# A gated linear-attention and GEGLU kernel: another fixed order, with SyncE's issue of each DMA planned as a step, weights loaded in nine pieces, and a choice of engine for two elementwise steps

## Chip, cores, metric

One core of one Trainium2 chip; the calls of this study ran on different chips. The metric is the device time of one execution in microseconds (us), lower is better. Spans in traces are 1.7 us shorter than the device time of the same execution.

## The reference

Four batches of eight heads, 768 steps, head dimension 48. A complex-gated linear recurrence gives y, and y (3072 x 384) goes through a GEGLU block.

```python
mag = np.sqrt(a_re * a_re + a_im * a_im)
scale = np.minimum(mag, 0.999) / (mag + 1e-06)
for t in range(S):
    new_re = ar * S_re - ai * S_im
    new_im = ar * S_im + ai * S_re
    S_re, S_im = (new_re + k_t v_t^T, new_im)      # written short
    y[:, :, t] = q_t . S_re
g, val = x @ w_gate, x @ w_val                     # x is y, 384 -> 1536
return (gelu(g) * val) @ w_out                     # 1536 -> 384
```

## The kernel before

The kernel works in 24 chunks of 128 steps (six a batch) and in 8 units of three chunks (half a batch) for the gates. Log and angle of the gates are summed along time with triangular matrices on TensorE, turned into exponentials, sines and cosines, multiplied into q and k, and a chunk is then ordinary masked attention plus a state. Everything stands in one order, PLAN: each word is a step, a number after "=" is the buffer it writes, V or A the engine (VectorE or ScalarE). Each engine runs its own steps strictly in the order of the words.

```python
PLAN = """
ldare0=0 ldare1=1 tab.LE la0 ldaim0=0 r0=0 la1 ldaim1=1 r1=1 z0 ldv1=0 ldqk0=0 sq0 z1 ln0 vb1=0 ldqk2=1 sq1
...   # cut
gel4.0=1 g0.1=6 h2.1 g4.2=3 ldv8=1 h2.2 gel0.1=2 v4.0=5 pr5=2 gel4.1=0 tp6.0=0 ldqk9=3 sc3.1=6 v4.1=2
tps6.0A=0 h4.0=2 g0.2=4 ssb3.1=2 gel4.2=1 qk7=1 v4.2=5 vb8=7 tpd5.0=2 tp6.1=0 h4.1 y3.1 g0.0=6 tps6.1A=3 pr7=1
tpd5.1=1 v0.1=3 st6A=0 h4.2 sc6.0=2 x3A=1 v0.0=0 gel0.2=0 ssb6.0=1 ldv7=2 xtp3=5 gel0.0=1 v0.2=1 xt3A=1 h0.0=3
ldwo@qk9 sc6.1=4 y6.0=2 g3.1=6 ssb6.1=0 g3.0=5 h0.1 gel3.1=1 y6.1 sc5.0=0 h0.2 gel3.0=2 vb7=1 g3.2=4 x6A=0
...   # cut; dw7 stands in the next line
"""
FAST = (0, 1, 2, 3, 4, 5, 6,)     # units whose gates are loaded three steps a partition, in one DMA
SQUARES = (4, 6,)                 # units that take log(re^2 + im^2); the others log re and log(1 + (im/re)^2)

def load_weight(nm, after):       # "ldwo@qk9": w_out, behind the load of q and k of chunk 9
    t, src = WEIGHTS[nm]
    ...                           # cut: a one-column GpSimd copy that waits for the named load
    nc.gpsimd.dma_start(out=t, in_=src.rearrange("(c p) f -> p c f", p=128))

def si(u, slot, **_):             # im^2, for SQUARES
    nc.vector.tensor_tensor(out=take("s2", ("s2", u), slot), in0=T["aim", u], in1=T["aim", u], op=ALU.mult)

def vb(c, slot, **_):             # v to bf16
    nc.gpsimd.tensor_copy(out=take("vb", ("vb", c), slot), in_=T["v", c])

def tpd(c, hg, slot, **_):        # the pair of q and k of four heads, transposed by DMA
    src = T["pair", c][:, hg * 4:(hg + 1) * 4].rearrange("p h i s d -> p (h i s d)")
    nc.sync.dma_start_transpose(out=take("tps", ("tps", c, hg), slot), in_=src)

def dw(c, **_):                   # state update: pair^T v
    ...                           # cut: eight matmuls into the bank dwb, reading vb
```

Other words: la, r, sq, sr, ln are ScalarE steps of the gates (log, reciprocal, squares); z, ad, lx, mn VectorE ones; cum and cumt the sums on TensorE; ph, pg, sn phase, quarter turn and sine; tp a transpose on TensorE with copy tps; sc, ssb, y the attention; g, v, gel, h, fo, o the GEGLU block (g and v are its two up-projections, fo the down-projection); "tab.X" loads a table of ScalarE (LE log and exp, T arctangent and sine, G gelu); xtp or xtd transposes x on TensorE or by DMA.

Of the kernel before, what the change touches and what calls it, by code (L numbers as in the profile page):

```python
# [14 lines left out]
AF = mybir.ActivationFunctionType  # L15
ALU = mybir.AluOpType
# [9 lines left out]

PLAN = """
ldare0=0 ldare1=1 tab.LE la0 ldaim0=0 r0=0 la1 ldaim1=1 r1=1 z0 ldv1=0 ldqk0=0 sq0 z1 ln0 vb1=0 ldqk2=1 sq1
lx0=0 ln1 ldqk1=2 mn0 lx1=1 ldare3=0 tab.T at0=0 mn1 at1=1 cumt1=0 ldaim2=0 cumt0=1 ph1V=0 cumt5=2 pg1 ph0V=1
sn1=0 ldqk4=3 cumt2=3 pg0 ph5A=2 cumt3=4 sn0=1 pg5 cum0=5 ph3V=3 ph2A=0 cum4=6 sn5=2 ldqk6=4 pg2 cumt4=0 pg3  # L30
cum1=1 sn2=3 ph4V=1 cum5=2 sn3=4 cum2=3 pg4 ldaim3=1 cum3=4 sn4=5 tab.LE E0=0 ldare2=1 E2=1 qk0=0 E1=2 qk2=1
ldv0=1 E4=3 pr0=0 E5=4 ldv4=2 pr2=1 tp0.1=0 E3=5 ldwg@are2 la2 qk1=2 tp0.0=5 vb0=1 qk4=3 tp2.0=3 la3 vb4=2
pr1=2 dw0=0 r2=0 tp2.1=1 pr4=0 tps0.0A=0 z2 tp4.1=6 r3=1 sc0.0=2 tps2.1V=1 st0A=0 ssb0.0=0 sq2 tpd1.1=2
sc2.1=4 dw1 tps0.1V=3 tp4.0=5 st1A=1 y0.0=1 z3 sc0.1=2 ln2 tpd1.0=0 ssb0.1=1 sq3 lx2=0 y0.1 ldv3=3 tps2.0A=3
sc1.1=0 ldqk3=5 ssb2.1=2 x0A=0 sc2.0=2 mn2 ln3 ssb2.0=3 cum7=3 ssb1.1=0 sc1.0=4 cum8=1 E7=0 vb3=3 ldv2=4
ssb1.0=1 cum6=2 E8=1 lx3=1 y1.0=0 ldwv@v3 E6=2 y1.1 qk3=4 tps4.0V=0 vb2=4 tab.T at2=0 qk6=5 sc4.0=3 dw2 y2.0=4
pr3=2 at3=1 y2.1 cumt7=1 cumt8=2 ssb4.0=1 st2A=0 cumt6=5 ph7A=2 tps4.1V=2 dw3 ph8A=0 cumt9=3 ph6V=3 x1A=1
ldv6=5 cumt11=1 st3A=1 pg8 pg6 ph9A=1 sc4.1=6 xtp1=2 pg7 sn8=6 cumt10=0 tpd3.0=3 ssb4.1=0 dw4 y4.0=5 sn7=7
xt1V=0 x2V=1 y4.1 g1.1=3 ph10A=0 mn3 ldaim4=0 pg9 sn6=1 g1.0=6 vb6=5 ph11V=2 sn9=3 xtp2=2 pg10 g1.2=4 pg11
xt2V=1 sn10=0 v1.0=0 pr6=1 ldqk8=0 sn11=5 sc3.0=1 g2.2=2 x4V=1 st4V=1 g2.0=5 ssb3.0=3 dw6=0 ldqk5=1 si4=0  # L40
tab.G gel1.0=0 v1.1=1 gel1.1=1 v2.0=6 gel1.2=2 h1.0=0 g2.1=3 ldv5=0 qk8=6 gel2.2=0 v1.2=4 h1.1 xtd0=2 xtp4=0
v2.2=2 xt4A=0 pr8=0 tpd3.1=1 y3.0=1 gel2.0=1 v2.1=0 h1.2 g4.0=5 vb5=6 h2.0=1 gel2.1=2 ldqk7=2 g4.1=4 qk5=0
gel4.0=1 g0.1=6 h2.1 g4.2=3 ldv8=1 h2.2 gel0.1=2 v4.0=5 pr5=2 gel4.1=0 tp6.0=0 ldqk9=3 sc3.1=6 v4.1=2
tps6.0A=0 h4.0=2 g0.2=4 ssb3.1=2 gel4.2=1 qk7=1 v4.2=5 vb8=7 tpd5.0=2 tp6.1=0 h4.1 y3.1 g0.0=6 tps6.1A=3 pr7=1
tpd5.1=1 v0.1=3 st6A=0 h4.2 sc6.0=2 x3A=1 v0.0=0 gel0.2=0 ssb6.0=1 ldv7=2 xtp3=5 gel0.0=1 v0.2=1 xt3A=1 h0.0=3
ldwo@qk9 sc6.1=4 y6.0=2 g3.1=6 ssb6.1=0 g3.0=5 h0.1 gel3.1=1 y6.1 sc5.0=0 h0.2 gel3.0=2 vb7=1 g3.2=4 x6A=0
ssb5.0=3 v3.0=3 gel3.2=0 xtp6=6 v3.1=1 h3.0=4 sc5.1=5 xt6V=0 tp8.0=2 h3.1 v3.2=0 ssb5.1=2 y5.0=4 tps8.0V=0 dw7
tp8.1=3 ldare5=1 h3.2 y5.1 sc8.0=6 g6.1=1 st7A=1 tps8.1V=3 g6.2=5 x5V=1 gel6.1=2 ssb8.0=1 g6.0=2 tpd7.0=2
gel6.2=1 v6.1=0 gel6.0=0 xtp5=3 v6.0=4 tpd7.1=1 xt5A=2 sc8.1=1 g5.0=6 h6.0=5 ssb8.1=0 v6.2=5 ldare4=0 gel5.0=0
h6.1 g5.2=2 g5.1=3 h6.2 gel5.2=2 v5.0=4 gel5.1=1 ldqk10=5 v5.2=1 h5.0=6 v5.1=6 cum9=0 tab.LE la5 h5.1 ldaim5=1  # L50
fo0=5 h5.2 E9=3 r5=0 qk9=2 cum10=2 ldqk11=4 fo4=3 o0V=0 la4=1 pr9=2 E10=5 z5 ldqk12=0 r4 fo6=4 o4A=1 qk10=3
sq5 ldqk13=1 z4 fo3=6 o6A=2 sr4 pr10=1 ldout4 ln5 cum11=1 ad4 ldv10=3 fo1=0 E11=2 ldaim6=0 lx5=0 ln4=1 dw8
y8.0=5 qk11=4 tp10.0=2 o3A=1 y8.1 vb10=0 sc7.1=3 tps10.0A=0 mn5 tp10.1=4 ldv11=4 mn4 cum15=1 ssb7.1=3 st8A=1
cum17=6 ldv9=5 x8A=0 tps10.1V=3 cum16=2 E15=1 pr11=0 cum13=3 ldv17=0 E17=4 cum14=5 si6=0 cum12=4 vb11=4 xtd8=1
E16=0 fo2=1 ldv16=1 E12=3 vb9=2 E13=5 ldout6 qk12=5 vb17=3 ldout0 E14=2 sc7.0=6 sc10.0=2 qk13=6 sc10.1=4
ldaim7=1 fo5=3 ssb7.0=2 vb16=5 ssb10.1=1 tab.T at5=0 ssb10.0=0 y7.0=5 dw9 o2V=2 at4=1 y7.1 cumt16=6 o1V=0
ldv13=2 cumt17=4 st9V=0 ph16A=3 cumt15=2 tpd9.0=2 x7A=1 ph17V=1 y10.0=1 cumt14=0 ph15A=0 pg16 pg17 tp11.0=6
sn16=4 pg15 tp11.1=5 ph14V=2 ldv12=3 sn17=1 cumt13=4 vb13=6 tps11.0V=1 cumt12=2 ldout1 sn15=6 tps11.1V=0
xtp7=0 sc11.0=6 ldqk16=2 y10.1 pg14 ph12A=3 dw10 xt7V=0 g8.0=5 ph13A=1 ssb11.0=2 sn14=2 g7.0=2 pg12 vb12=7
pg13 o5A=0 sc11.1=0 x10V=0 ldv21=4 g7.2=4 sn13=7 ssb11.1=3 g8.2=6 sn12=3 ldv14=5 pr13=0 v8.0=3 xtd10=2 qk16=0  # L60
g7.1=1 ldqk15=3 v7.0=0 pr12=1 tab.G gel7.0=0 vb21=1 gel7.2=1 g8.1=2 h7.0=3 st10A=0 vb14=0 v7.1=4 gel7.1=2
tpd13.0=3 gel8.0=0 v8.2=0 h7.1 dw12=0 v7.2=1 h8.0=2 gel8.2=2 ldqk14=5 sc9.0=5 gel8.1=0 qk15=1 g10.0=4 y11.0=3
h7.2 v8.1=6 ssb9.0=0 tpd9.1=1 gel10.0=1 y11.1 v10.0=2 h8.1 x11A=1 y9.0=1 st12V=0 g10.1=5 h8.2 tpd13.1=0
xtp11=4 dw13 gel10.1=0 v10.1=3 qk14=2 g10.2=6 xt11V=0 ldqk17=4 h10.0=5 g11.2=0 gel10.2=2 pr16=2 g11.0=5
gel11.2=1 sc9.1=4 h10.1 g11.1=2 ldare7=1 ssb9.1=1 gel11.0=0 v11.2=6 pr14=0 y9.1 v11.1=0 st13A=1 qk17=3 x9A=0
sc13.0=3 v11.0=4 ssb13.0=2 xtp9=5 tpd12.1=2 dw14 v10.2=1 h11.0=4 sc13.1=3 xt9V=1 gel11.1=0 y13.0=4 h10.2
g9.0=5 tpd12.0=1 ssb13.1=3 g9.1=2 gel9.0=2 h11.1 g9.2=1 tpd14.1=3 h11.2 gel9.1=0 y13.1 v9.0=3 x13V=1 st14A=0
gel9.2=1 sc12.1=5 v9.1=0 h9.0=0 ldout5 ssb12.1=0 xtp13=2 tpd14.0=0 v9.2=6 xt13A=0 h9.1 sc12.0=4 g13.0=1 pr15=1
ldqk23=0 g13.2=3 gel13.0=2 ssb12.0=1 g13.1=5 gel13.2=0 h9.2 y12.0=2 v13.2=0 gel13.1=1 tpd15.1=1 y12.1 sc14.1=1
pr17=0 sc14.0=4 x12A=0 v13.0=3 ssb14.0=2 xtp12=6 v13.1=5 ldv15=0 xt12V=2 y14.0=2 ssb14.1=3 g12.1=4 ldv18=1  # L70
h13.0=1 g12.0=6 tpd15.0=2 h13.1 gel12.1=2 y14.1 g12.2=1 x14A=1 h13.2 vb15=4 gel12.0=1 v12.0=3 gel12.2=0
ldare6=0 xtp14=4 v12.2=5 h12.0=6 vb18=2 xt14A=1 v12.1=2 g14.1=0 h12.1 ldqk22=1 g14.2=6 gel14.1=1 h12.2 g14.0=1
gel14.2=2 fo8=3 gel14.0=0 ldout2 ldqk18=2 v14.1=4 tab.LE la7 o8V=0 v14.0=2 la6=0 tpd17.0=0 sc15.1=0 fo9=5
h14.0=2 ssb15.1=1 r7=1 h14.1 ldqk21=3 sr6 z7 fo7=6 r6 ad6 ldout3 sq7 fo13=1 ldqk19=5 o9V=2 z6 ln6=0 v14.2=3
ldout8 ln7 o13V=1 ldv22=2 fo12=2 mn6 h14.2 ldout13 lx7=1 ldqk20=4 cum18=0 cum19=4 o7V=0 E18=3 sc15.0=5 mn7
vb22=6 cum20=1 o12V=1 E19=5 ldv20=3 cum22=3 ssb15.0=0 cum23=6 E20=0 qk18=4 cum21=0 ldout12 dw15 fo14=2 E22=1
tpd16.0=3 qk19=6 st15A=1 qk22=5 E21=2 vb20=7 ldout9 y15.0=4 E23=4 qk20=0 fo10=5 tpd16.1=2 qk21=2 qk23=1 y15.1
tab.T at7=0 ldout7 fo11=1 o10V=1 tpd17.1=1 at6=1 x15V=0 o14V=2 sc16.0=3 xtd15=0 dw16 o11A=0 cumt22=0 ssb16.0=2
st16A=0 ldout14 sc17.0=6 cumt21=5 ph22A=0 cumt23=4 ssb17.0=3 ldv23=4 ph21A=2 sc16.1=2 pg22 cumt18=1 ph23A=1
pg21 sn22=0 ldout10 cumt19=3 ssb16.1=0 y16.0=0 ldout11 pg23 sn21=5 y17.0=5 cumt20=6 ph19V=3 ldv19=5 y16.1  # L80
sn23=7 ph18V=0 g15.0=4 vb23=0 pg19 ph20A=2 g15.2=2 x16V=1 sn19=3 pg20 sc17.1=3 xtd16=2 g15.1=1 pg18 sn20=4
ssb17.1=1 v15.2=6 pr19=1 sn18=2 vb19=4 y17.1 v15.1=0 x17V=0 tpd19.0=3 v15.0=3 pr18=2 g16.2=5 tab.G gel15.0=0
pr21=0 gel15.2=1 dw18=0 tpd19.1=0 g16.0=4 gel15.1=2 h15.0=0 v16.2=2 st18A=1 h15.1 gel16.2=0 v16.0=1 tpd18.0=2
h15.2 gel16.0=2 dw19 g16.1=3 st19V=0 fo15=5 xtd17=1 h16.0=3 gel16.1=1 tpd18.1=1 pr20=1 sc19.1=0 sc19.0=4
o15A=2 v16.1=6 ssb19.1=2 ldout15 ssb19.0=3 g17.1=1 h16.1 dw20 y19.0=3 gel17.1=2 v17.1=5 tpd20.1=3 h16.2
g17.2=0 pr23=2 y19.1 g17.0=4 gel17.2=1 x19V=1 tpd21.1=0 st20A=1 v17.2=6 gel17.0=0 sc18.1=1 sc18.0=2 dw21
ssb18.1=0 xtd19=0 fo16=0 ssb18.0=1 v17.0=3 o16V=1 sc21.1=4 y18.0=1 ldout16 h17.0=1 g19.0=2 tpd20.0=2 ssb21.1=3
g19.2=0 gel19.0=0 h17.1 v19.0=3 h17.2 gel19.2=2 y18.1 g19.1=4 tpd21.0=1 x18V=0 fo17=2 h19.0=6 gel19.1=1
xtd18=2 pr22=1 sc20.0=5 v19.2=0 o17V=0 v19.1=6 ssb20.0=2 ldout17 sc20.1=1 sc21.0=4 h19.1 y20.0=3 g18.0=2
# [8 lines left out]
ldout22 o23A=0 ldout23  # L98
"""

FAST = (0, 1, 2, 3, 4, 5, 6,)

SQUARES = (4, 6,)


@with_exitstack
def kernel(
# [148 lines left out]
    def si(u, slot, **_):  # L256
        nc.vector.tensor_tensor(out=take("s2", ("s2", u), slot), in0=T["aim", u], in1=T["aim", u],
                                op=ALU.mult)
# [223 lines left out]
```

## Time and profile before

| | before |
|---|---|
| time, median of the runs ahead of the prediction | 250.13 us (249.15 to 250.96) |
| profiled execution | 252.22 us, span 250.5 us |
| PE, DVE, ACT busy | 85%, 75%, 66% |
| DMA queue of SyncE | 140,032 packets, 38.4 MB, 80% of 16 engines' span |

The lines themselves are in the prediction. To read them: PE busy is not PE's useful work (at half clock the same matmuls are busy twice as long), so the prediction adds up the work at full clock, 197.5 us, and asks where the other 53 us of the span went. The profiled execution is labelled slow, which on one core means only that it is over 1.5% above the fastest run; no die or clock is set apart by it. What the slower runs have in common is looked at in the experiments.

### The profile page before, as it was taken

To read this page: it belongs to the slowest core of one execution; us is meant where nothing else is said; L and a number is where in the kernel's file an instruction comes from. 1 tells how busy PE (TensorE), PEld (TensorE's weight loads), DVE (VectorE), ACT (ScalarE), POOL (GpSimd) and SP (SyncE) were. 2 spreads that over 40 slices of the span, in tenths; PEclk is the share of its full clock that TensorE was granted. 3 is DMA by queue.
4 is the path that set the end of the run, shared out by engine and by line. 5 is a ranking of instruction groups with operands and counts; after the bars stand their busy time and mean duration, and the time that the engine had idled before them with its cause. 6 is when DMAs were issued, how large, how long until landed. Compare 5 with 4: busy or idle time off the path is not lost.

```text
span 250.5 us, 7144 instructions
## 1 busy us (share of the span) xinstructions
PE 211.8 (85%) x3006; PEld 178.3 (71%) x3006; DVE 186.9 (75%) x306; ACT 164.4 (66%) x256; POOL 27.2 (11%) x56
## 2 busy tenths in 40 slices
PE   0029267699997499999989999999999999999994
PEld 0015165479997497566889999866679888888892
DVE  4466699989997236999999997399979868454360
ACT  4998999898663049999894465796889321443221
POOL 8100311500110000033130000000000000000000
PEclk9999755789999689999999999999999999999999
DMA  7999799998979999579899999999975756873011
GB/s 206 277 261 221 198 185 190 182 226 163 185 116 187 156 220 228 117 182 225 179 190 149 203 175 159 221 194 256 194 194 97 152 119 132 133 85 100 16 34 63
DMA packets 142416, 42.41 MB, mean 169 GB/s; under 512 B 122672, under 2 KB 141616, under 8 KB 142384
## 3 DMA queue, kind: packets, MB, share of 16 engines
q1 hardware_dynamic: 140032, 38.42, 79.8%
q0 software_dynamic: 2352, 3.54, 8.6%
q8 instruction: 23, 0.38, 0.6%
q14 instruction: 9, 0.07, 0.1%
HBM read 30.67 MB, written 4.72 MB: 141 GB/s over the span
## 4 chain that ended last, share of the span: by engine, by line
PE 61%; DMA 13%; ACT 10%; DVE 8%; issue 3%; SPq 2%; POOL 0%; DVEq 0%; POOLq 0%
PE bank L400 30%; PE bank L423 16%; PE bank L288 6%; DMA v<-in_v_dram 5%; ACT cs L316 3%; PE bank L352 3%; DMA aim<-in_a_im_dram 3%; ACT L441 2%; DMA out_dram<-o 2%; DVE z L248 2%; DMA tps<-pair 2%; DVE qke L320 2%; DVE pair L329 1%; PE bank L368 1%; PE dwb L373 1%
## 5 line engine op out<-in xcount | busy, mean ns | idle before, releaser
L410 ACT ACTIVATE gel<-bank 128x512 bf16<-128x512 f32 x72 | 42.3, 600 | 46.9 <-PE bank L400 28.3
L416 DVE TENSOR_TENSOR h<-bank,gel 128x512 bf16<-128x512 f32 x72 | 48.0, 687 | 19.3 <-PE bank L400 18.8
L400 PE MATMUL bank<-xt,wg 128*128 128x128 bf16 x864 | 57.2, 222 | 1.5 <-ACT gel L410 1.1
L400 PE MATMUL bank<-xt,wv 128*128 128x128 bf16 x864 | 57.3, 219 | 0.0
L400 PEld LDWEIGHTS <-wg 128*128 128x128 bf16 x864 | 51.3, 99 | 1.9 <-issue 1.9
L400 PEld LDWEIGHTS <-wv 128*128 128x128 bf16 x864 | 50.4, 98 | 0.8
L423 PE MATMUL bank<-wo,h 128*128 128x384 bf16 x288 | 49.9, 326 | 0.0
L423 PEld LDWEIGHTS <-h 128*128 128x128 bf16 x288 | 27.4, 98 | 16.7
L355 DVE TENSOR_TENSOR ssb<-bank,tri 128x512 bf16<-128x512 f32 x48 | 32.3, 684 | 3.5 <-PE bank L352 3.3
L324 POOL CAST vb<-v 128x384 bf16<-128x384 f32 x24 | 18.0, 753 | 141.4 <-DMA v<-in_v_dram 112.4
L288 PEld LDWEIGHTS <-cum 128*128 128x128 bf16 x126 | 13.1, 108 | 27.0 <-issue 19.4
L288 PE MATMUL bank<-th,cum 128*128 128x384 bf16 x63 | 15.0, 388 | 17.7 <-ACT th L277 17.4
L329 DVE TENSOR_TENSOR pair<-qke,cs 128x768 bf16<-128x768 bf16 x48 | 25.8, 584 | 1.7 <-DMA tps<-pair 1.0
L320 DVE TENSOR_TENSOR qke<-qk,e 128x768 bf16<-128x768 f32 x24 | 23.3, 996 | 4.5 <-ACT e L299 3.6
L352 PE MATMUL bank<-tps 128*128 128x128 bf16 x192 | 19.2, 232 | 3.1 <-DVE tps L208 2.5
L316 ACT ACTIVATE cs<-ph 128x768 bf16<-128x768 int16 x24 | 18.9, 848 | 1.2 <-DVE ph L311 1.1
L352 PEld LDWEIGHTS <-tps 128*128 128x128 bf16 x192 | 13.5, 103 | 5.4 <-DVE tps L208 2.8
L338 PE MATMUL bank<-ident,pair 128*128 128x128 bf16 x112 | 11.0, 264 | 6.5 <-DVE pair L329 6.5
L368 PE MATMUL bank<-vb,ssb 128*128 128x48 bf16 x192 | 15.5, 187 | 0.9 <-DVE ssb L355 0.8
L441 ACT ACT_TABLE_LOAD x11 | 14.1, 1283 | 1.0 <-PEq L466 0.8
L298 ACT ACTIVATE e<-bank 128x384 bf16<-128x384 f32 x24 | 12.8, 532 | 2.8 <-PE bank L288 2.8
L208 ACT CAST st<-dwb 128x384 bf16<-128x384 f32 x16 | 7.9, 491 | 9.9 <-PE bank L368 9.4
(63 smaller groups left out, 248.9 us busy)
## 6 DMA issues: line engine op xcount, KB each, us to landing
v<-in_v_dram SPq DMA_DIRECT2D x24, 192.0 KB, 4.0
qk<-in_q_dram SPq DMA_DIRECT2D x24, 192.0 KB, 4.5
qk<-in_k_dram SPq DMA_DIRECT2D x24, 192.0 KB, 4.4
out_dram<-o SPq DMA_DIRECT2D x24, 192.0 KB, 2.6
are<-in_a_re_dram SPq DMA_DIRECT2D x7, 576.0 KB, 5.5
aim<-in_a_im_dram SPq DMA_DIRECT2D x7, 576.0 KB, 5.5
wg<-in_moe_w_gate_dram POOLq DMA_DIRECT2D x1, 1152.0 KB, 8.7
wv<-in_moe_w_val_dram POOLq DMA_DIRECT2D x1, 1152.0 KB, 9.9
```

Of the source, the lines that this page charges most:

```text
L288: nc.tensor.matmul(ps, mat, xin[:, :, c2, :], start=(n == 0), stop=(n == len(srcs) - 1))
L316: act(out=take("cs", ("cs", c), slot).rearrange("p s h d -> p (s h d)"), in_=lo[:, :, 0], func=AF.Sin, scale=2.0 * PI / TURN)
L320: nc.vector.tensor_tensor(out=take("qke", ("qke", c), slot), in0=T["qk", c], in1=T["e", c], op=ALU.mult)
L329: nc.vector.tensor_tensor(out=pair[:, :, i, :, 0:D], in0=T["qke", c][:, i].unsqueeze(2).to_broadcast([128, H, 2, D]), in1=T["cs", c].rearr ...
L352: nc.tensor.matmul(ps[:, hi, :], t[:, 2 * hi + 1, :], t[:, 2 * hi, :], start=True, stop=True)
L355: nc.vector.tensor_tensor(out=take("ssb", ("ssb", c, hg), slot), in0=T["sc", c, hg], in1=tri.unsqueeze(1).to_broadcast([128, 4, 128]), op= ...
L368: nc.tensor.matmul(ys, T["ssb", c, hg][:, hi, :], T["vb", c][:, h, :], start=first, stop=True)
L400: nc.tensor.matmul(ps[:, fi * L:(fi + 1) * L], w[:, i, fc * 128:(fc + 1) * 128], T["xt", c][:, i, :], start=(i == 0), stop=(i == NDM - 1))
L410: act(out=take("gel", ("gel", c, f), slot).rearrange("p a t -> p (a t)"), in_=T["g", c, f], func=AF.Gelu)
L416: nc.vector.tensor_tensor(out=T["h", c][:, f * FW:(f + 1) * FW, :].rearrange("p a t -> p (a t)"), in0=T["val", c, f], in1=T["gel", c, f].r ...
L423: nc.tensor.matmul(ps, T["h", c][:, fc, :], wo_sb[:, fc, :], start=(fc == 0), stop=(fc == NFF - 1))
L441: nc.scalar.preload_act_table_set(TABLES[word[4:]])
```

## The change

The intent: a planner that treats each DMA's issue on SyncE as a step with a duration makes the order, so that loads are not planned for times at which SyncE is still busy with other DMAs. It may also put the square of im and the quarter turn on either engine. Each weight is loaded in three pieces, other units take the log of re^2 + im^2 (SQUARES) or leave the interleaved load (FAST), and the new plan has 25 table loads in place of 11. The core of the diff (the plan is cut to its beginning):

```diff
 PLAN = """
-ldare0=0 ldare1=1 tab.LE la0 ldaim0=0 r0=0 la1 ldaim1=1 r1=1 z0 ldv1=0 ldqk0=0 sq0 z1 ln0 vb1=0 ldqk2=1 sq1
-lx0=0 ln1 ldqk1=2 mn0 lx1=1 ldare3=0 tab.T at0=0 mn1 at1=1 cumt1=0 ldaim2=0 cumt0=1 ph1V=0 cumt5=2 pg1 ph0V=1
+ldare0=0 ldaim0=0 ldare1=1 ldaim1=1 ldqk2=0 ldqk1=5 tab.LE la0=0 r0 ldqk0=4 sr0 z0 si0V=0 la1 ad0 ldaim2=0
+r1=1 ldqk3=3 ln0=0 z1 ldqk5=2 mn0 sq1 cum2=0 ln1 cum0=6 ldv0=0 cum1=5 E2=0 lx1=1 E0=5 ldqk4=1 E1=4 qk0=0
 ...   # cut: all other lines of the plan differ as well
-FAST = (0, 1, 2, 3, 4, 5, 6,)
-SQUARES = (4, 6,)
+FAST = (0, 1, 2, 3, 5,)
+SQUARES = (0, 2, 5, 6,)
-    def load_weight(nm, after):
+    def load_weight(nm, f, after):
         t, src = WEIGHTS[nm]
+        src = src.rearrange("(c p) f -> p c f", p=128)
+        if nm == "wo":
+            t, src = t[:, f * FW:(f + 1) * FW, :], src[:, f * FW:(f + 1) * FW, :]
+        else:
+            t, src = t[:, :, f * FW * 128:(f + 1) * FW * 128], src[:, :, f * FW * 128:(f + 1) * FW * 128]
-    def si(u, slot, **_):
+    def si(u, slot, eng):         # cut: eng "A" squares on ScalarE
-    def pg(c, **_):
+    def pg(c, eng, **_):          # cut: eng "A" turns on ScalarE
```

All 24 quarter turns and all four squares of the new plan stand on VectorE, so that choice is not used.

## The prediction

> **What bounds the kernel now.** I read four views of the kernel before, in this order. First the page's first two parts, busy shares and slices:
>
> ```profile
> PE 211.8 (85%) x3006; PEld 178.3 (71%) x3006; DVE 186.9 (75%) x306; ACT 164.4 (66%) x256; POOL 27.2 (11%) x56
> PE   0029267699997499999989999999999999999994
> ACT  4998999898663049999894465796889321443221
> PEclk9999755789999689999999999999999999999999
> DMA  7999799998979999579899999999975756873011
> ```
>
> PE is nearly full from the tenth slice (6.26 us each) to the end, with one hole in slices 13 and 14. So the bound is: a head of some 55 us in which PE has little to do, then PE itself. In the head ACT is at 9. To see what PE's work is worth without waits I took its durations from the chain: 12 matmuls of one up-projection group take 0.67 us, 12 of a down-projection 1.95, three of a 384-wide cumulative sum 0.49, eight transposes 0.45, four of a score 0.22, eight of a state update 0.20, and so on. By the plan's counts that is 144 x 0.67 + 24 x 1.95 + 138 x 0.163 + 14 x 0.45 + 48 x 0.22 + 20 x 0.20 + some 9 + 2 = 197.5 us. The span is 250.5, so 53 us are lost to PE. The stages show where (the columns after the stretch's length are PE, weight loads, DVE, ACT, POOL, then clock, DMA share, GB/s):
>
> ```profile
> 0.00:17.00 17.00, 0.00 (x0) 0.10 (x1) 9.47 (x13) 12.65 (x11) 6.61 (x27) 1.00 1.03 240
> 17.00:55.00 38.00, 27.07 (x243) 18.70 (x243) 30.12 (x49) 34.66 (x53) 6.95 (x9) 0.73 1.07 203
> 55.00:78.00 23.00, 23.00 (x432) 22.94 (x429) 21.83 (x39) 17.01 (x29) 2.29 (x4) 1.00 0.96 167
> 78.00:90.00 12.00, 7.14 (x101) 7.05 (x99) 4.55 (x9) 1.67 (x3) 0.51 (x1) 0.72 1.01 163
> 90.00:160.00 70.00, 68.91 (x1064) 59.83 (x1062) 60.48 (x98) 51.72 (x87) 8.81 (x11) 1.00 1.02 186
> ```
>
> Up to the first up-projection at 55.0 us only 18.6 us of the 197.5 are done: 36.4 us are lost there. The stretch 78 to 90 loses most of the rest; after 90 us PE is busy but for some 2 us, and the tail after the last matmul costs 3.6. Third, the waits of PE:
>
> ```profile
> PE bank L288 <- ACT th L277: 17.4, 1, 17.4
> PE bank L338 <- DVE pair L329: 6.5, 2, 4.9
> PE dwb L373 <- POOL vb L324: 4.9, 1, 4.9
> PE bank L352 <- DVE tps L208: 2.5, 2, 2.0
> ```
>
> The first two are the head: PE waits 17.4 us for the first arctangent and later for the first pair. The third is the hole. Fourth, the chain of work over the hole:
>
> ```profile
> 70.94 0.69 PE bank L400 x12
> 71.63 0.55 SPq L345
> 72.23 11.66 DMA v<-in_v_dram
> ...
> 84.02 0.52 POOL vb L324
> 84.54 0.04 issue
> 84.58 0.48 PE dwb L373 x8
> ```
>
> It is the load of v7: SyncE is in the middle of a transposing DMA (L345) until 72.2, only then issues v7, and this load lands after 11.66 us where the median is 4.0, because the weight load of w_out was issued at 70.97 and takes 12.7. PE waits 4.86 us and then runs at half clock: the eight matmuls of dw take 0.48 us instead of 0.20, the next eight transposes 0.85 instead of 0.45, the 48 up-projections 4.15 instead of 2.68. With the y and score matmuls between (some 0.4) that is 4.9 + 2.5 = **7.4 us lost to one late load**.
>
> **What the Trainium skill says.** "TensorE: Matmul & The Clock Gate", section "HAM oscillation — how this bites in real kernels": a PE gap longer than about 3.4 us brings the slow clock back. The trace agrees: clock 0.53 in 84 to 90 us after the 4.86 us wait, and 0.50 in 30 to 42 after the 4.9 us wait for the pair. "DMA: Bandwidth & Descriptors", section "Issuing engines are not separate DMA queues": transfers of all issuers share the same 16 DMA engines and interleave. The trace agrees: v7 took 11.66 us beside a 1152 KB weight load. "ScalarE: Activation LUTs", section "What ACT_TABLE_LOAD costs": about 1283 ns, plus a drain of about 1380. This trace has the first figure (11 loads, mean 1283 ns) but no second: the load at 14.89 us is followed by the arctangent at 16.18.
>
> **The change, part by part.** (1) The loads are placed earlier. I counted, for each load, the PE work that stands in the order between it and its first consumer. For v the median goes from 3.0 us to 9.1, for q and k from 6.1 to 13.5, for a_im from 4.1 to 7.2. v7, which stood 2.8 us ahead of its cast and 6.7 ahead of its matmul, now stands 11.3 and 36.2 ahead. In the order up to that matmul, six transposing DMAs of the pair become two, so SyncE isn't held by waits for pairs. The weights come in nine pieces of 384 KB instead of three of 1152, each behind some other load, so none can hold the DMA engines for 12 us. I expect the hole to go: **-7.4 us**.
>
> (2) Head. Units 0 and 2 now take the log of re^2 + im^2, so the first sum of logs doesn't wait for the quotient and its square: by the ACT and DVE durations (1.16 and 1.36 us) I get the first PE work near 13 us instead of 17.4, the exponentials of chunks 0 to 2 before the first table change, and the first pair near 23 to 25 instead of 29.2. The bound of this stretch is ACT, which ran some 4 us behind its own sum of durations before (51.0 us of work at 55.0). Before the first up-projection the new order has 48.3 us of ACT work against 51.0, with 19.9 us of PE work done against 18.6: ahead by 2.7 + 1.3 = 4. But at the first gelu table it has 55.3 against 53.5, with 26.1 of PE against 21.9: ahead by 2.4. And DVE has 52.4 us of work up to that place, against 44.2, because of the squares and adds of units 0 and 2 and the copies of transposes that PE now makes; it starts near 6 us and waits for ACT some 4 us, so both engines arrive at about 60 with no slack between them. I take **-1.5 us**.
>
> (3) PE's own sum. Units 4 and 6 leave the interleaved form: 138 cumulative matmuls become 126, -12 x 0.163 = -2.0 us. Pair transposes on PE go from 14 to 18, +4 x 0.45 = +1.8; those of x from 12 to 8, -4 x 0.17 = -0.7. Sum **-0.9 us**.
>
> (4) Table loads go from 11 to 25: 14 x 1.28 = +17.9 us on ACT, and the copies that move add nearly nothing. The new ones lie in pairs around single sines, logs or exponentials amid the gelus. There ACT has slack: from the second gelu stretch to the last a-units, 37.7 us of PE work stand beside 34.4 us of ACT. But each pair holds the gelus up for about 2.6 to 3.7 us while seven banks fill, so some of the seven new visits will cost PE some tenths. I take **+2.0 us**. DVE gains about 2 x (1.36 + 1.36 - 1.40) = 2.6 for squares plus some copies, beside PE.
>
> The choice of engine for quarter turn and square is not used by this plan: all of both stand on VectorE, so it costs nothing. The leave of the interleaved form adds 8 plain DMAs with short rows (q, k and v have the same rows and land in 4 us); they have much lead.
>
> Sum: 250.1 - 7.4 - 1.5 - 0.9 + 2.0 = 242.3, and I put 242.5.
>
> **The rivals.** First: another load is late in place of v7. For it: the DMA engines are already at 9 in most slices of the first 180 us, and the new order asks for 12.3 MB in place of 11.7 by the time 20 us of PE work are done, which at 215 GB/s is 57 us; the first piece of w_gate hangs behind q and k of chunk 6. Against: the leads above. If it comes, 5 to 8 us return: 247 to 250. Second: ACT becomes the bound amid the gelus. For it: 25 loads and a sum of 192 us by durations against 175. Against: in both orders the stretches where ACT is full (before: 96 to 126 and 161 to 190 us) have no more ACT work than before. If it does: +4 to +6, some 247. Third: the head follows its ACT sum fully and the extra tables hide: 237 to 239.
>
> **Range and chances.** The hole is sure to have cost 7 us, the head can go 4 us either way, table loads from 0 to 6. Range 236 to 249. Faster by over 2% means under 245.1: 0.68. Within 2%: 0.28. Slower: 0.04.
>
> **What would show it.** In the profile after: no PE wait for vb above 1 us and no clock under 0.9 after 60 us (part 1); first matmul near 13 us and first up-projection near 53 (part 2); 126 cumulative matmuls, 144 pair transposes (part 3); 25 table loads, and PE idle in front of gelus (waits of L400 on gel, now 1.1 us) of 2 to 4 us (part 4). A wait of several us on a load or on a weight piece, or ACT at 9 between 130 and 160 us, would prove me wrong.

## The result, and the profile after

The changed kernel took 243.05 us in the median (241.97 to 243.19, 4 runs) against 250.5 us (249.15 to 250.96) for the kernel before on the same chip. The ratio of the fast runs is 0.970, 95% interval 0.965 to 0.975. A ratio is the mean time of one kernel's fast runs over that of the other's of the same rounds, so not quite the ratio of the medians quoted. All four runs of before counted as fast there; the experiments show that this was the slower of two groups into which its runs fall.

The page of the changed kernel, busy shares and slices (6.03 us each):

```profile
PE 208.3 (86%) x3014; PEld 174.2 (72%) x3014; DVE 188.4 (78%) x308; ACT 180.5 (75%) x270; POOL 31.0 (13%) x68
PE   0058834999999999998999979999799999999993
ACT  3897899899769569699979869798899772333230
PEclk9999995699999999999999999999999999999999
DMA  7999999999897999999997999999957897601212
```

The hole of slices 13 and 14 is gone, PE's clock is full from the ninth slice on, and PE is at 5 in the third slice, where it was at 2. ACT is busier, 180.5 us against 164.4. The stages, cut as before (columns: length, then PE, weight loads, DVE, ACT and POOL with counts, clock, DMA share, GB/s):

```profile
0.00:17.00 17.00, 3.04 (x9) 1.38 (x10) 10.45 (x14) 12.41 (x15) 5.75 (x26) 1.00 1.02 243
17.00:55.00 38.00, 27.82 (x297) 19.78 (x297) 34.36 (x59) 34.95 (x53) 11.59 (x18) 0.87 1.12 221
55.00:78.00 23.00, 22.04 (x404) 21.48 (x403) 22.94 (x37) 19.53 (x29) 6.30 (x10) 1.00 0.89 167
78.00:90.00 12.00, 12.00 (x204) 11.24 (x202) 7.87 (x14) 6.92 (x12) 1.88 (x4) 1.00 1.14 179
90.00:160.00 70.00, 67.59 (x1011) 57.27 (x1009) 58.29 (x96) 61.34 (x93) 4.97 (x9) 1.00 1.03 189
```

In 78 to 90 us PE went from 7.14 to 12.00 us busy, with the clock from 0.72 to 1.00. In 55 to 78 it is DVE that is full, 22.94 of 23. The waits of PE (us in total, times, longest):

```profile
PE bank L299 <- DVE lx L285: 16.3, 3, 13.2
PE bank L382 <- DVE ssb L369: 3.1, 1, 3.1
PE bank L380 <- ACT st L211: 2.0, 1, 2.0
PE bank L366 <- DMA tps<-pair: 1.9, 2, 1.7
PE bank L414 <- DMA xt<-x: 1.3, 1, 1.3
```

The wait for vb is not among them. The first wait now ends at 13.2 us with a sum of logs, where the first arctangent ended it at 17.4. No wait for a gelu shows; transposing DMAs (3.2 us) are new.

Loads do still land late. The landings of the q and k loads, of before and then of the changed kernel:

```profile
DMA to landing us min/median/max: 3.2/4.4/6.3
```

```profile
DMA to landing us min/median/max: 3.1/4.0/11.5
```

By the trace, four of them, issued between 43.0 and 46.3 us, took 8.3 to 11.5 us while pieces of w_gate and w_val were under way. With the lead that they have here VectorE waited 0.4 us for one q or k load in the whole run, and PE for none.

To say what each stage gave, take one mark that both have, the first down-projection. It is the start in the first line of the tile w_out (min, median and max ns, first and last start in us), here of before and then of the changed kernel:

```profile
L423 PE MATMUL bank<-wo,h x288: 322/326/326, 96.9 to 246.5; 128*128 128x384 bf16 x144
```

```profile
L437 PE MATMUL bank<-wo,h x288: 322/326/326, 88.5 to 237.1; 128*128 128x384 bf16 x144
```

By the durations in the prediction 51.7 us of PE work stand ahead of that mark in the order before and 52.8 in the new one, so 45.2 and 35.7 us were lost up to it: 9.5 us less. After the mark, before loses 153.6 - 145.8 = 7.8 us and the changed kernel 152.7 - 143.8 = 8.9: 1.1 us more. With 0.9 us less work in all that is 9.5 - 1.1 + 0.9 = 9.3 us, the difference of the spans.

### The profile page after: what moved, and what is told of

The parts are those of the page before. It is cut to its first block, busy times and chain, and to the rows that moved or that the text cites. A ratio compares the mean times of both kernels' runs of the same rounds, so it can differ in the third digit from the quotient of the medians.

```text
span 241.2 us, 7177 instructions
## 1 busy us (share of the span) xinstructions
PE 208.3 (86%) x3014; PEld 174.2 (72%) x3014; DVE 188.4 (78%) x308; ACT 180.5 (75%) x270; POOL 31.0 (13%) x68
## 4 chain that ended last, share of the span: by engine, by line
PE 60%; DVE 15%; ACT 10%; DMA 5%; issue 3%; SPq 1%; DVEq 0%; ACTq 0%
PE bank L414 32%; PE bank L437 15%; PE bank L299 6%; DMA tps<-pair 4%; PE bank L366 3%; DVE ssb L369 3%; DVE qke L334 2%; ACT e L310 2%; DVE pair L343 2%; ACT e L309 2%; DVE h L430 2%; DVE tps L211 1%; ACT L455 1%; ACT th L288 1%; ACT cs L330 1%
## 5 line engine op out<-in xcount | busy, mean ns | idle before, releaser
L424 ACT ACTIVATE gel<-bank 128x512 bf16<-128x512 f32 x72 | 40.9, 599 | 35.1 <-PE bank L414 16.7
L430 DVE TENSOR_TENSOR h<-bank,gel 128x512 bf16<-128x512 f32 x72 | 47.7, 685 | 17.9 <-PE bank L414 10.8
L414 PEld LDWEIGHTS <-wg 128*128 128x128 bf16 x864 | 50.2, 98 | 2.7 <-DMA xt<-x 1.4
L455 ACT ACT_TABLE_LOAD x25 | 32.1, 1283 | 1.2 <-PEq L480 0.8
L299 PEld LDWEIGHTS <-cum 128*128 128x128 bf16 x90 | 9.6, 115 | 25.1 <-issue 19.6
L299 PE MATMUL bank<-lx,cum 128*128 128x384 bf16 x45 | 12.8, 415 | 16.3 <-DVE lx L285 16.3
L338 POOL CAST vb<-v 128x384 bf16<-128x384 f32 x24 | 14.1, 618 | 97.6 <-DMA v<-in_v_dram 84.6
L343 DVE TENSOR_TENSOR pair<-qke,cs 128x768 bf16<-128x768 bf16 x48 | 24.4, 551 | 0.4 <-ACT cs L330 0.4
L366 PE MATMUL bank<-tps 128*128 128x128 bf16 x192 | 17.7, 222 | 3.3 <-DMA tps<-pair 1.9
L366 PEld LDWEIGHTS <-tps 128*128 128x128 bf16 x192 | 12.4, 99 | 6.1 <-DMA tps<-pair 3.7
L382 PEld LDWEIGHTS <-ssb 128*128 128x128 bf16 x192 | 12.0, 98 | 6.3 <-DVE ssb L369 3.5
L380 PE MATMUL bank<-st,tps 128*128 128x48 bf16 x160 | 13.9, 186 | 2.0 <-ACT st L211 2.0
```

Of the source, the lines that this page charges most:

```text
L299: nc.tensor.matmul(ps, mat, xin[:, :, c2, :], start=(n == 0), stop=(n == len(srcs) - 1))
L343: nc.vector.tensor_tensor(out=pair[:, :, i, :, 0:D], in0=T["qke", c][:, i].unsqueeze(2).to_broadcast([128, H, 2, D]), in1=T["cs", c].rearr ...
L366: nc.tensor.matmul(ps[:, hi, :], t[:, 2 * hi + 1, :], t[:, 2 * hi, :], start=True, stop=True)
L382: nc.tensor.matmul(ys, T["ssb", c, hg][:, hi, :], T["vb", c][:, h, :], start=first, stop=True)
L414: nc.tensor.matmul(ps[:, fi * L:(fi + 1) * L], w[:, i, fc * 128:(fc + 1) * 128], T["xt", c][:, i, :], start=(i == 0), stop=(i == NDM - 1))
L424: act(out=take("gel", ("gel", c, f), slot).rearrange("p a t -> p (a t)"), in_=T["g", c, f], func=AF.Gelu)
```

## The experiments

Words of the plan are moved unless said otherwise. Times are medians of all runs; the runs of before that shared the chip are given beside them.

### One load earlier

```diff
-... vb8=7 tpd5.0=2 ... tpd5.1=1 ... ssb6.0=1 ldv7=2 xtp3=5 ...
+... vb8=7 ldv7=2 tpd5.0=2 ... tpd5.1=1 ... ssb6.0=1 xtp3=5 ...
```

> The order of before with one word moved: the load of v7 stands ahead of the first transposing DMA of chunk 5 instead of behind the second, some 7 us of PE work earlier. Theory of the prediction (one late load cost 7.4 us): v7 issues near 67 us, lands before the w_out load starts, PE does not wait for vb, the clock stays 1.0 in 78 to 90 us, and the time falls by 6 to 8 us to some 243. Rival (the DMA engines are full and the hole only moves to another load or transpose): 247 or more, with a new PE wait of some us between 70 and 100 us.

Measured: 246.54 us (245.05 to 247.7, 4 runs), but before itself ran at 246.53 in the median there, 245.37 to 250.59 in 8 runs; the ratio of fast runs is 1.00, unclear. In the trace the hole is gone, as the stage and the tile w_out show:

```profile
78.00:90.00 12.00, 12.00 (x219) 11.60 (x217) 8.30 (x15) 6.81 (x10) 0.00 (x0) 1.00 1.25 209
```

```profile
L418 PE MATMUL bank<-wo,h x288: 322/326/326, 89.4 to 240.6; 128*128 128x384 bf16 x144
```

The longest landing of a v load fell from 11.7 to 6.5 us, and the first down-projection came 7.5 us earlier, at 89.4. The span is 5.9 us shorter than in the trace of before (244.6 against 250.5): 1.6 us were given back to other waits after the mark. So the mechanism stands. The time is not the 243 us that was expected and equals that of before, which was quick in five of its eight runs there. The likely reading, not shown, is that the hole is missing in those five.

### The weight later

```diff
-... h0.0=3 ldwo@qk9 sc6.1=4 ... gel3.0=2 vb7=1 g3.2=4 ...
+... h0.0=3 sc6.1=4 ... gel3.0=2 vb7=1 ldwo@v7 g3.2=4 ...
```

> The order of before, v7 issued as late as there, but the 1152 KB load of w_out hangs behind v7 instead of behind chunk 9's q and k. If the contention with w_out made v7 late (prediction): v7 lands in some 4 us near 76, no PE wait for vb, some 243 to 245. Rival (SyncE's late issue alone is the cause, or transposes hold the engines as well): v7 still takes over 8 us and the time stays at 248 to 250. A third way: w_out now comes late for the first down-projection at 97 us; then a PE wait on L423 shows.

Measured: 246.64 us (244.92 to 249.39, 4 runs), the same runs of before. SyncE issued v7 at 72.33 as late as before, behind the same two transposing DMAs; its cast ran at 75.44, so it had landed within 3.2 us:

```profile
72.33 0.58 SPq L213 DMA_DIRECT2D v<-in_v_dram  x1
75.44 0.51 POOL L319 CAST vb<-v 128x384 bf16<-128x384 f32 x1 [4.03 <-PE bank L395]
```

No wait for vb, first down-projection at 89.3, none for w_out. So it takes both: SyncE's late issue alone does no harm, and beside w_out v7 lands 7 to 9 us later. That is the prediction's reading, though the time is again above the 243 to 245 expected. One of the four runs took 249.39 us; it was not profiled, so what made it slow is open.

### The weight in three pieces at the same place

```diff
-ldwg@are2 ... ldwv@v3 ... ldwo@qk9
+ldwg0@are2 ldwg1@are2 ldwg2@are2 ... ldwv0@v3 ldwv1@v3 ldwv2@v3 ... ldwo0@qk9 ldwo1@qk9 ldwo2@qk9
```

(with the change's load_weight)

> The order of before with each weight loaded in three pieces of 384 KB as in the change, but all three pieces at the place of the whole. The same bytes at the same time: by the prediction v7 shares the engines with them as before, takes 9 to 12 us, and the time stays at 249 to 251. Rival (it is the size of one transfer that holds v7 back): v7 lands in under 7 us, PE waits less than 2 us, and the time falls to some 244.

Measured: 250.46 us (246.81 to 251.25, 4 runs). The time is what the prediction expected and the reason is not: no v load took over 6.8 us, as the rival said. What was lost is elsewhere. GpSimd issues the weights, a piece of w_gate takes it 1.7 us or more (a one-column copy and 0.8 to 0.9 us of issue), and three of them in a row hold the cast of v0 and v4 from 30.6 to 35.2 us. PE waits 2.6 us for vb in the head (1.6 behind the pieces of w_gate, 1.0 behind those of w_val), and the first up-projection starts at 57.4 instead of 55.0:

```profile
PE dwb L373 <- POOL vb L324: 2.6, 2, 1.6
```

v7 was issued 0.08 us behind the first piece of w_out and landed in 5.8 us; a load of a_re issued 0.6 us later still took 12.1 us (12.4 in before). So smaller pieces saved v7 here, not every load, and they cost GpSimd's queue; the time cannot be attributed to either alone.

### Whole weights in the new order

```diff
-... ldwg1@v1 ... ldwg2@v2 ... ldwv0@v9 ... ldwg0@qk6 ... (nine pieces)
+... ldwg@v1 ... ldwv@v9 ... ldwo@v10 ... (three weights whole, with the load_weight of before)
```

> The changed kernel with each weight loaded whole, at the place of the first of its three pieces. If the greater lead of the loads protects it (prediction): within 1 or 2 us of the changed kernel, 243 to 245, with no PE wait on vb over 1 us. Rival (spreading the weights in thirds is what removed the hole): a PE wait on a load of 4 us or more and 247 to 250.

Measured: 243.99 us (241.88 to 245.43, 4 runs). One v load (v9, whose issue began 0.4 us ahead of w_gate's) took 11.3 us here too. GpSimd holds w_val and the casts behind it until v9 has landed, and PE waited 0.5 us for a cast:

```profile
DMA to landing us min/median/max: 3.0/3.9/11.3
```

```profile
PE dwb L376 <- POOL vb L327: 0.5, 1, 0.5
```

The lead of the loads is enough to remove the hole; the splitting of the weights is not needed for it.

### The kernel before, once more

> The kernel before, unchanged, for a second trace: its runs so far lie from 245 to 252 us. If the late load of v7 is what tells its quick executions from its slow ones, a profiled run under 247.5 us shows no PE wait for vb over 1 us and a v7 landing in under 7 us, and one over 249 us shows the wait of some 5 us again. If the spread has another cause (clock, head), the wait is there in both.

The profiled run was of the slower group again (251.71 us). Its chain of work:

```profile
73.26 0.55 SPq L345
73.87 10.17 DMA v<-in_v_dram
...
84.16 0.52 POOL vb L324
84.72 0.41 PE dwb L373 x8
```

The same late load, with a PE wait of 3.4 us. The 68 timed runs of before in this study fall in two groups: 28 between 245.1 and 248.0 us (median 246.4), 37 between 249.0 and 253.3 (median 250.3), three between. The kernel with v7 earlier took 245.1 to 247.7 in its four runs, which is the quicker group. Both profiles of before fell in the slower group and show the hole. A quick execution was never profiled, so that the quick ones lack the hole is inferred from the edit, not seen. In the two traces w_out is issued at 70.97 and 73.32 us, 1.3 and 0.6 us before v7. That is close, but no trace shows the order turned round, and v9 above was late though its issue began 0.4 us ahead of w_gate's. One run with w_out later took 249.39 us as well. So what tells the two groups apart is not shown: the late load is the likely cause, and perhaps not the only one.

The label slow (over 1.5% above the fastest run) falls on most of the slower group, so the ratio of fast runs compares with the quick group almost alone whenever a quick run is present.

### The changed kernel on the same chip as the next two

> The changed kernel, unchanged, on the same chip as the others of this call. Expected 242 to 243.5 with a spread of 1.5 us, as in the first result. Against the quick runs of before (some 246.5) that is a ratio near 0.985; against its slow ones (250.5) 0.970. If the gain were all the one late load, it would show no gain over the quick runs of before.

Measured: 244.12 us (243.25 to 245.99, 6 runs); ratio of fast runs 0.9875, interval 0.980 to 0.995, because only the quick runs of before (247.0 in the mean) count as fast there. The time is above the 242 to 243.5 expected. The interval leaves out 1, so the gain is not all the one late load. Over all its 68 runs before has a mean of 248.8 us; the ten runs of the changed kernel have 243.7. So the change is worth some 7 us against the slower group, some 3 against the quick one, and the spread is smaller: 4 us in ten runs against 8 in 68.

### The quotient again in the first units

```diff
-SQUARES = (0, 2, 5, 6,)
+SQUARES = (5, 6,)
-... la0=0 r0 ldqk0=4 sr0 z0 si0V=0 la1 ad0 ldaim2=0 r1=1 ldqk3=3 ln0=0 z1 ...
+... la0 r0=0 ldqk0=4 z0 sq0 la1 r1=1 ldqk3=3 ln0 lx0=0 z1 ...      (unit 2 alike)
```

> The changed kernel with units 0 and 2 by the quotient again, as in before (square and log of 1 + z^2 instead of the log of the sum of squares). Prediction: first PE work comes near 17 us instead of 13, but VectorE saves 2 x 1.3 us in a head where it is full; ScalarE's sum is unchanged. I expect +0.5 to +2 us over the changed kernel, 243.5 to 245. Rival (VectorE alone bounds 30 to 74 us, the early start of PE is worth nothing): 1 to 3 us faster than the changed kernel, 240 to 242.

This try was faulty: it left the load of unit 2's im ahead of the last use of its buffer, gave wrong values (relative error 0.055) and took 256.82 us. It says nothing. The second moved ldaim2 behind lx0:

> The quotient for units 0 and 2 again, now with the next a_im load placed behind the last use of its buffer (the first try had it ahead, gave wrong values and waited for the load). Prediction as there: first PE work near 17 us instead of 13, +0.5 to +2 us over the changed kernel of this call. Rival (VectorE bounds the head, and the 2.6 us it saves count): 1 to 3 us faster.

Measured: 250.41 us (248.99 to 253.8, 6 runs), correct, ratio of fast runs over before 1.012 where the changed kernel has 0.9875: some 6 us slower, three times the top of what I expected. First PE work came at 16.6 us instead of 13.3, as expected, but more was lost behind it. The profiled run was the slowest of the six (253.8 us, labelled slow), so its waits may be larger than in the others. VectorE's waits in the first 45 us, of this kernel and then of the changed one on the same chip:

```profile
DVE lx L276 <- ACT aim L273: 6.8, 2, 4.6
```

```profile
DVE lx L281 <- ACT aim L278: 2.1, 1, 2.1
```

VectorE stands idle for the log of 1 + z^2 on ScalarE, and since it works in order, the pairs and masks behind it wait too; unit 2's log then comes so late that PE waits another 6.3 us for it at 49 us. So in this order the squares are worth far more than the 1.3 us of VectorE that each costs: they break the chain ScalarE, VectorE, ScalarE, ScalarE, VectorE. The rival (VectorE's sum bounds the head) falls. One reserve: in this kernel the load of unit 2's im is some steps later and no planner has arranged the rest for the quotient, so 6 us is what the squares are worth in this order, not in the best order without them.

### The table loads

Doubled: each of the seven visits to another table amid the gelus is made twice, with no work in the second.

```diff
-... tab.T sn16=3 ... tab.G ...
+... tab.T tab.G tab.T sn16=3 ... tab.G ...      (seven times)
```

> The changed kernel with each of its seven visits to another table amid the gelus made twice: 14 more table loads of 1.28 us, 39 in all, +18 us on ScalarE, same work otherwise. Prediction: the first seven visits cost PE some 2 us together, so seven more of the same length cost 2 to 4: 245 to 247. Rival (ScalarE has become the bound amid the gelus): most of the 18 us show, 252 or more. Other rival (fully hidden): within 0.5 us of the changed kernel.

Freed: wrong values on purpose.

```diff
-act(..., func=AF.Sin, ...)      act(..., func=AF.Ln)
+act(..., func=AF.Copy if c in (15, 16, 20, 21, 22) else AF.Sin, ...)   AF.Copy if u in (5, 6, 7) else AF.Ln
-tab.T ... tab.G      (the seven visits)
```

> Wrong values on purpose: the changed kernel with the five sines and three logs of its seven visits computed as plain copies of the same shapes, so that the visits need no table and 14 loads (18 us of ScalarE) go; 11 stay, as in before. This is the cost of the visits by itself. Prediction: some 2 us faster than the changed kernel of this call. Rival by the doubling (+12.5 us for 14 loads, so some 0.9 us a load): 6 to 12 us faster. Other rival (hidden until doubled): within 0.7 us.

Measured: without the 14 loads 243.07 us (242.13 to 244.1, 6 runs; fast-run ratio 0.982) against 244.12 for the changed kernel in the same rounds: 1.0 us for 18 us of ScalarE (1.2 in the means; an estimate from the six runs of each gives a 95% interval of 0.1 to 2.3). With 14 more loads 255.47 us (255.19 to 256.22, 4 runs, on another chip): some 11 to 12 us over the changed kernel's two medians, for the same 18 us; the run with squares on GpSimd (below), on the same chip, took 242.67. The stages tell why, first without the 14, then the changed kernel, then with 14 more:

```profile
130.00:150.00 20.00, 18.64 (x335) 17.58 (x332) 15.08 (x23) 10.42 (x18) 1.93 (x4) 1.00 1.02 175
190.00:210.00 20.00, 20.00 (x336) 17.67 (x333) 14.22 (x26) 8.05 (x16) 0.00 (x0) 1.00 0.75 133
```

```profile
130.00:150.00 20.00, 18.45 (x329) 17.39 (x325) 15.53 (x24) 16.96 (x23) 2.60 (x4) 1.00 1.01 180
```

```profile
130.00:150.00 20.00, 14.36 (x245) 13.15 (x243) 10.85 (x17) 19.82 (x23) 1.93 (x4) 1.00 0.99 166
190.00:210.00 20.00, 16.16 (x244) 13.45 (x241) 12.32 (x23) 17.61 (x23) 0.00 (x0) 0.97 0.73 132
```

In 130 to 150 us ScalarE has 10.4 of 20 us of work without the visits, 17.0 in the changed kernel, and is full (19.8) with them doubled; PE goes from 18.6 over 18.5 to 14.4. The change spent more than half of ScalarE's slack in this stretch, nearly free, and seven more visits spent the rest. My +2 to 4 for seven more does not hold; my +2 for the first seven is too high by the medians, but within the noise.

### The sines in one group

```diff
-... sn14=4 ... tab.G ... tab.T sn16=3 ... tab.G ... tab.T sn15=5 ... tab.G ...
+... sn14=4 sn16=3 sn15=5 ... tab.G ...          (sn20, sn21, sn22 likewise, with ph22 and pg22; eight loads fewer)
```

> The changed kernel with the sines of chunks 15, 16, 20, 21 and 22 moved to the earlier group of sines, so that four visits (eight table loads, 10.3 us of ScalarE) go; 17 loads stay. The result stays right. Prediction: four visits cost some 1.2 us, the five sines put ahead of the gelus give part of it back: 241.5 to 244. Rival (table visits eat the gain of the order): 238 to 240. Other rival (the visits are what lets the gelus start in time): 245 or more.

Measured: 247.92 us (245.34 to 250.24, 20 runs on one chip), 4 us over the changed kernel's medians elsewhere and 5 over the next run, on the same chip, with 10 us less work on ScalarE. The profiled run, 245.93 us, is one of the quicker of the twenty. The second rival is right: the sines put ahead make the gelus start late. In 170 to 190 us PE is busy 14.87 of 20 us (18.28 in the changed kernel's second trace), and it waits for a gelu there:

```profile
PE bank L408 <- ACT gel L418: 3.0, 1, 3.0
PE bank L360 <- DMA tps<-pair: 2.2, 1, 2.2
```

In this order the extra loads are the price of having gelus first, and it pays.

### Squares on GpSimd

```diff
-nc.vector.tensor_tensor(out=t, in0=T["aim", u], in1=T["aim", u], op=ALU.mult)
+(nc.gpsimd if eng == "P" else nc.vector).tensor_tensor(...)      # si2P, si5P, si6P
```

> The changed kernel with the squares of a_im of units 2, 5 and 6 on GpSimd instead of VectorE (3 x 1.36 us off VectorE). If VectorE bounds the stretch 46 to 74 us, as its unbroken run in the chain of the changed kernel says, the square of unit 5 at 60 us is on the path: 1 to 1.5 us faster, some 241.5 to 242. Rival (GpSimd is slow at it and the sum of squares, or VectorE beside it, waits): 243 to 246.

Measured: 242.67 us (242.05 to 244.46, 4 runs), correct. That is 0.4 us under the changed kernel's first median and 1.5 under its second, on a third chip; within the spread, so it is not shown to be faster. A square takes 2.36 us on GpSimd against 1.35 on VectorE. No run here gave a version that is shown to beat the changed kernel.

## Why the prediction was right, and where it was not

- **The number**: 242.5 foreseen, 243.05 and later 244.12 measured, both inside the range. The forecast of over 2% held against the runs of before that it was made from; against the quick ones the gain is 1.2%. That the sum came so near is partly luck, since two errors cancel: the hole was put too large for the end time and the rest too small. Taking out the hole alone took 5.9 us off the span, and 3.7 off the median (slower group of before to v7 earlier), not 7.4. The changed kernel lies some 3 us below that, on other chips, where parts 2 to 4 together had -0.4.
- **Part 1, the late load, -7.4 us**: the mechanism is right. Moving that one load took 7.5 us off at the mark of the first down-projection. Two things were missing. Of the 7.5 us, 1.6 were lost again by the end of that kernel. And I took the hole for a property of every execution from one trace; the two groups of times speak against that, but how often it strikes is not shown. Against the quick group the change gains 3 us, not 7.
- **Part 1, why the new order is safe**: right about the lead (a landing of 11.3 us cost 0.5 us). Wrong that pieces of 384 KB cannot hold other loads up so long: q and k loads took up to 11.5 us beside them. By the run with whole weights the split added nothing.
- **Part 2, the head, -1.5 us**: at the mark, the changed kernel had lost 35.7 us and before without the hole 37.7 (89.4 - 51.7), so -2.0. First PE work at 13.2 us, first pair at 23.8 and first up-projection at 53.1 came where they were foreseen (13, 23 to 25, 53), and VectorE was the full engine from 55 to 78. What the squares are worth was underrated: undoing them costs 6 us.
- **Part 3, PE's own sum, -0.9 us**: the counts are as foreseen, 126 cumulative matmuls and 144 pair transposes. No run took it by itself.
- **Part 4, table loads, +2.0 us**: 25 loads as foreseen, but 1.0 us (0.1 to 2.3). The sign I named for it was wrong: PE has no wait for a gelu at all. The other sign, ScalarE at 9 between 130 and 160 us, did come in part (25.7 of 30 us busy, at 9 in three slices that touch it) and did no harm: PE was busy 28.5 of the 30. The 1.1 us more lost after the mark shows as waits for transposing DMAs, 3.2 us, which I had not in the sum.
- **Rivals**: other loads did come late, but PE waited for none of them. ScalarE did not become the bound amid the gelus, but the doubled visits show that it was within seven visits of it. In before ScalarE was less full from 161 to 190 us than the prediction says: 25.0 of 29 us.

By the traces the sum is -7.5 (hole) -2.0 (head) -0.9 (work) +1.1 (after the mark) = -9.3 us against a forecast of -7.8. The traced execution of before was a slow one of its group.

## What to carry to other kernels

Look at the lead of each load, in work of the engine that would wait, and not only at whether it is hidden in one trace: v7, with 3 us of lead beside a large transfer, was late in both traces, and moving one word settled it. Repeat the kernel before often enough to see whether its times fall in two groups; a ratio against one group is not the gain. Here seven visits to another table amid the gelus cost some 1 us while ScalarE had slack there, and seven more some 12; ask for the slack of the stretch, not for the price of a load.

## What the Trainium skill lacked or had wrong

- "ScalarE: Activation LUTs", section "What ACT_TABLE_LOAD costs": it gives about 1283 ns for the load, which the traces agree with (25 loads, mean 1283 ns), and a drain of about 1380 ns on top. None shows: in the changed kernel a load starts at 29.79 us, right behind the last sine, and the exponential behind it at 31.08; 14 loads more or less move ScalarE's busy time by 17.9 us (162.4 to 180.3), 1.28 each. It doesn't say how little or how much of a load shows in the time of a kernel (1.0 and some 12 us for 14).
- "DMA: Bandwidth & Descriptors", section "Issuing engines are not separate DMA queues", calls the sequencer's time to start a DMA usually small relative to the DMA. Here the 24 v loads held SyncE for 0.75 us in the median and up to 2.65 beside landings of 4.0. The two transposing DMAs ahead of v7 held it for 3.98 us: 1.3 and 1.2 of their own and 1.5 of waiting between them, which is how v7 came to be issued late. Nor does it say for how long an issue holds GpSimd's queue: 0.7 to 0.9 us a piece here.
- The same section says that transfers interleave. How late a small load then lands is missing: a 192 KB load issued 0.6 and 1.3 us behind a 1152 KB one landed after 10.2 and 11.7 us instead of 4.0, and one issued 0.4 us ahead of one after 11.3.
- "TensorE: Matmul & The Clock Gate", section "HAM oscillation — how this bites in real kernels": agrees, as near as it can be told: after a wait of 3.37 us in the second trace of before the eight matmuls of dw took 0.41 us instead of 0.20.
